# Fused forgetting attention and GELU MLP on one core: batch 2 in the order of the later batches

## The chip, the cores and the metric

The kernel runs on one core of a Trainium2 chip. The metric is device time in microseconds (us), the median of several runs. The engines are called as the profile calls them: PE (TensorE, matmuls), PEld (its weight loads), DVE (VectorE), ACT (ScalarE), POOL (GpSimd) and SP (SyncE). SP computes nothing here: its queue issues the DMAs of the outputs, of v, and all DMA transposes. POOL's queue issues the loads of q, k and the weights.

## The reference, cut to what matters

Two operations stand behind each other. The first is causal attention with a decay from a forget gate, the second a two-layer MLP with an exact GELU on its output.

```python
batch, n_heads, seq, head_dim = (8, 8, 576, 64)

def attention(q, k, v, f):
    B, H, S, D = q.shape
    scores = np.matmul(q, k.transpose(0, 1, 3, 2)) / np.sqrt(D)
    cum = np.cumsum(np.log(np.clip(f, 0.0001, 1.0)), axis=-1)
    decay = cum[:, :, :, None] - cum[:, :, None, :]
    causal = np.triu(np.ones((S, S), dtype=bool), k=1)
    scores = np.where(causal, -1000000000.0, scores + decay)
    scores = scores - np.max(scores, axis=-1, keepdims=True)
    attn = np.exp(scores)
    attn = attn / (np.sum(attn, axis=-1, keepdims=True) + 1e-09)
    return np.matmul(attn, v)

def mlp(x, w_in, w_out):             # x: 4608 tokens x 512, d_ff = 2048
    h = x @ w_in
    g = 0.5 * h * (1.0 + erf(h / np.sqrt(2.0)))
    return g @ w_out

a = attention(q, k, v, f)
out = mlp(a.transpose(0, 2, 1, 3).reshape(B * S, H * D), w_in, w_out)
```

## The kernel before, in words

The work goes batch by batch (b = 0 to 7), with the order of all instructions written out by hand. Of the 576 rows of a batch, 512 (TC) go through the MLP as one chunk; the other 64 (TL), its *tail*, are gathered over all eight batches in the tile `tails`, and go through the MLP together at the end.

A batch consists of these steps. `load_qk_tokens` (POOL's queue) and `load_v` (SP's queue, five DMAs) bring q, k and v. `transpose_dma` has SP transpose q and k of four heads into the tiles `tq` and `tk`, and `untangle` has DVE copy them into `qT[i]` and `kT[i]`, one pair of heads `i` at a time (L269). `weigh_v` multiplies v with the decay on POOL (L288). `scores(b, i, t)` computes four tiles of scores for a pair of heads (L319), takes their exponential on ACT (L329) and masks the diagonals on POOL (L331). `attend` multiplies with v (L350), `normalize` divides on DVE, and `x_dma` has SP transpose the result into `xT` (L397). The name "av" below stands for `attend` and `normalize` of a pair of heads, with its `x_dma`. `gemm1` is the first layer (L447) with the GELU on ACT (L467), 16 blocks of four matmuls.

The second layer of a batch is computed during the attention of the next one, as filling between the score tiles. It is a generator, and `take(fill, n)` runs `n` of its steps. In `gemm2_rows` (L551) a step is either one matmul over 128 rows ("n") or two matmuls of 64 rows that write two PSUM banks ("r"), which DVE then adds up (L565 copies one, L575 adds the other, L579 stores). A plan lists for each of four row blocks (`ts`) the PSUM pool that holds its banks and its 16 steps.

Batches 3 to 7 have one order: all 16 score tiles with filling between them (`FILL`), then `av(0)`, `av_both(1)`, `av_both(2)`, `av(3)`, four steps of filling, the tail (`tail` with 40 matmuls of L416, `tail_end` with a divide on DVE and a transpose on SP, L429), the rest of the filling, and `gemm1_open`, which opens seven PSUM banks as the transposed x of the four pairs arrive.

Batches 0 and 1 have orders of their own that the change leaves alone. Batch 2, too, has its own order. Its filling is longer by 48 steps (`gemm2_third`: 16 steps of `gemm2_second`, L615, and 32 of `PLAN_0` finish batch 0; then come 64 steps of batch 1 by `PLAN_1`). The av of pair `i - 1` stands behind the second score tile of pair `i`. It attends to five blocks of rows instead of four; the fifth holds the tail, which `x_tail` copies out of `xT` on POOL (L435). gemm1 opens with five blocks.

PSUM comes from three pools of two buffers each: `s_psum` (two banks a buffer, tag "s", scores), `o_psum` ("o") and `m_psum` ("m"). The pool `x_pool` has four buffers for each tag; the four x of a batch and the x of `tail_end` share the tag "x".

Of the kernel before, what the change touches and what calls it, by code (L numbers as in the profile page):

```python
# [54 lines left out]
def kernel(  # L55
# [18 lines left out]
    XC = NBLK * P  # L74
    TL = S - TC
    assert B * TL == TC
# [281 lines left out]
    def normalize(b, i, h):  # L358
        if (b, i) not in x_of:
            x_of[b, i] = x_pool.tile([P, NBLK, 2, D], BF16, tag="x", name="x")  # L360
        nm = blocks(b)
        divide(x_of[b, i][:, 0:nm, h, :], o_of[b, i, h], nm)

    def blocks(b):
        return NBLK if b in (0, 2) else NBLK - 1
# [11 lines left out]
    def xT(b):  # L377
        if b not in xT_of:
            xT_of[b] = xT_pool.tile([P, n_dm, XC], BF16, tag="xT", name="xT")
        return xT_of[b]  # L380

    def to_xT(b, i, copy, pool=m_psum, tag="m", ps=None):
        if ps is None:
            shape = [P, 2, 1024] if pool is s_psum else [P, XC]
            ps = pool.tile(shape, BF16, tag=tag, name="ps_x")
            if pool is s_psum:
                ps = ps[:, 0, 0:XC]
        nm = blocks(b)
        for m in range(nm):
# [3 lines left out]
        copy(xT(b)[:, i, 0 : nm * P], ps[:, 0 : nm * P])  # L393

    def x_dma(b, i):
        nm = blocks(b)
        nc.sync.dma_start_transpose(  # L397
            xT(b)[:, i, 0 : nm * P].rearrange("d (m p) -> d m p", p=P),
            x_of[b, i][:, 0:nm].rearrange("p m h d -> p (m h d)"),
        )  # L400
# [24 lines left out]
    def tail_end(b, o):  # L425
        x = x_pool.tile([P, NBLK, 2, D], BF16, tag="x", name="x")
        x = x.rearrange("p k h d -> p (k h) d")[:, 0:HP]
# [5 lines left out]

    def x_tail(b):
        nc.gpsimd.tensor_copy(tails[:, :, b], by_half(xT(b)[:, :, XC - TL :]))  # L435

# [40 lines left out]
    def gemm2(c):  # L477
# [43 lines left out]
    PLAN_0 = [(2, "o", 16 * "r"), (3, "m", 14 * "r" + 2 * "n")]  # L521
    PLAN_1 = [
        (0, "m", 14 * "r" + 2 * "n"),
        (1, "m", 14 * "r" + 2 * "n"),
        (2, "m", 12 * "r" + 4 * "n"),
        (3, "s", 16 * "n"),
    ]
# [3 lines left out]
    def gemm2_rows(c, plan):  # L531
# [4 lines left out]
        for ts, held, steps in plan:  # L536
            if held == "s":
                both = s_psum.tile([P, 2, d_model], FP32, tag="s", name="ps2")
                banks = [both[:, 0], both[:, 1]]
            else:  # L540
                pool = {"o": o_psum, "m": m_psum}[held]
                banks = [
                    pool.tile([P, d_model], FP32, tag=held, name="ps2")
                    for _ in range(2)
                ]
            ot = o_pool.tile([P, d_model], FP32, tag="ot", name="ot")
            for kt, step in enumerate(steps):
                last = kt == steps.rfind("r")
                for r in range(2 if step == "r" else 1):
# [5 lines left out]
                        start=kt == (steps.index("r") if r else 0),  # L555
# [4 lines left out]
                if "r" in steps and (kt == n_ff - 1 if held == "s" else last):  # L560
# [5 lines left out]
                if kt == n_ff - 1:  # L566
                    if "r" in steps:
                        sum_out(c, ts, ot, banks[0])
                    else:
                        nc.vector.tensor_copy(ot, banks[0])  # L570
                        store(c, ts, ot)
# [55 lines left out]
    def gemm2_third():  # L627
        yield from gemm2_second(0)
        yield from gemm2_rows(0, PLAN_0)
        yield from gemm2_rows(1, PLAN_1)  # L630
# [7 lines left out]
    def behind(t, h):  # L638

        g = x_pool.tile([P, 1], FP32, tag="gate", name="gate")  # L640
        nc.gpsimd.tensor_copy(g[:PT], t[:, h, 0:1])
# [196 lines left out]
    def gemm1_begin(b, both):  # L838
# [3 lines left out]
        to_xT(b, HP - 1, nc.vector.tensor_copy, ps=both[:, 1, 0:XC])  # L842
# [15 lines left out]
    FILL_2 = [[8, 8, 8, 8], [8, 8, 4, 4], [4, 4, 4, 4], [4, 4, 4, 4]]  # L858

    def av_both(b, i):  # L860
# [3 lines left out]
        nm = blocks(b)  # L864
        both = st[:, :, 0 : nm * (D + 1)].rearrange("p h (m d) -> p h m d", m=nm)
        for h in range(2):
            o_of[b, i, h] = both[:, h]
            attend(b, i, h, range(nm))
        x_of[b, i] = x_pool.tile([P, NBLK, 2, D], BF16, tag="x", name="x")
        r = x_pool.tile([P, 2, nm], FP32, tag="r2", name="r2")  # L870
        nc.vector.reciprocal(r, both[:, :, :, D])
        nc.vector.tensor_tensor(
            x_of[b, i][:, 0:nm].rearrange("p m h d -> p h m d"),
            both[:, :, :, 0:D],
            r.unsqueeze(3).to_broadcast([P, 2, nm, D]),
# [24 lines left out]
    def attention(b):  # L900
# [5 lines left out]
        def av(i, n=0):  # L906
            for h in range(2):
                attend(b, i, h, range(blocks(b)))
                normalize(b, i, h)
                if h == 0:  # L910
                    take(fill, n)
            x_dma(b, i)

        for i in range(HP):
            for t in range(4):
                scores(b, i, t)
                take(fill, counts[i][t])
                if t == 1 and b == 2 and i > 0:
                    av(i - 1)
                    if i == 1:  # L920
                        load_v(3)
# [3 lines left out]
                if b > 2 and i == 0 and t == 1:  # L925
                    load_v(b + 1)
                if b > 2 and t == 0 and i < 2:
                    transpose_dma(b + 1, 4 * i, 4 * i + 4)
                if b == 2 and t == 1 and i == 1:
                    transpose_dma(3, 0, 4)  # L930
        if b == 2:
            take(fill, 4)
            av(HP - 1)
        else:
            av(0)
            av_both(b, 1)
# [165 lines left out]
```

## Time and profile before

| | |
|---|---|
| median of 3 runs | 329.86 us (329.84 to 330.63) |
| the profiled execution's own time | 330.98 us |
| its span, first to last instruction | 329.3 us |
| PE busy | 317.3 us (96%) |
| DVE, ACT, POOL busy | 179.6, 203.1, 131.2 us |
| mean granted clock of PE | 0.999 |
| batch 2, first score matmul to that of batch 3 | 67.86 to 113.31 us |

All durations come from one profiled execution. A timeline line gives the start in us, the length in us, the engine, the line of the program, the operation, output and inputs, the shape, and how many instructions were merged; in brackets stands the idle time before it and what ended it. The length of a matmul includes its way through the array, so matmuls that follow each other overlap in the timeline, and the pace of a stream is read from the starts. Some per cent of the matmul records are missing, so a count can be one or two short. A window line gives the window, its length, and for each engine the busy time with the number of instructions, then the clock, the share of the DMA engines and their rate.

### The profile page before, as it was taken

The page shows a single profiled execution, that of the slowest core. Times are in us where ns is not written, and L with a number is a line of the kernel's source. Part 1 is how long each engine was busy: PE and PEld are TensorE (multiplying, and loading weights), DVE is VectorE, ACT ScalarE, POOL GpSimd, SP SyncE. Part 2 cuts the span into 40 slices and gives each one's busy share as a digit, 9 for nine tenths or more (in the row PEclk, how much of TensorE's full clock was granted, in tenths as well). Part 3 has the DMA queues.
Part 4 walks back from the last instruction along what each step waited for, and adds up shares of the span by engine and source line. Part 5 has one row for each costly group of instructions (what it writes and reads, how often), then busy time and mean ns, then how long its engine had stood idle before and what let it go on. Part 6 is the DMA issues. An engine that isn't in the chain of part 4 may idle for free.

```text
span 329.3 us, 8075 instructions
## 1 busy us (share of the span) xinstructions
PE 317.3 (96%) x3291; PEld 168.9 (51%) x3323; DVE 179.6 (55%) x424; ACT 203.1 (62%) x296; POOL 131.2 (40%) x254
## 2 busy tenths in 40 slices
PE   7999799999999999999999999999999999999995
PEld 3664445445554456445644565455545564444443
DVE  5852566584458935792599449953795270010011
ACT  4896785984635797189808990899178936405600
POOL 8996883019426153804471356225512510000000
PEclk9999999999999999999999999999999999999999
DMA  7999999988998999499959794969610131021012
GB/s 114 190 192 211 207 189 124 185 176 144 196 220 180 146 201 199 74 158 170 218 76 175 141 222 95 176 120 202 129 41 3 66 82 56 0 88 42 0 47 83
DMA packets 94117, 43.93 MB, mean 133 GB/s; under 512 B 73344, under 2 KB 88960, under 8 KB 94080
## 3 DMA queue, kind: packets, MB, share of 16 engines
q1 hardware_dynamic: 76928, 26.90, 41.1%
q0 software_dynamic: 16752, 15.99, 30.8%
q8 instruction: 26, 0.43, 0.6%
q10 hardware_dynamic: 400, 0.52, 0.4%
q14 instruction: 11, 0.09, 0.1%
HBM read 36.85 MB, written 9.44 MB: 141 GB/s over the span
## 4 chain that ended last, share of the span: by engine, by line
PE 84%; DMA 9%; POOL 3%; issue 1%; ACT 1%; DVE 0%; another core or an unknown queue 0%; POOLq 0%; DVEq 0%
PE ps L447 35%; PE ps L551 26%; PE ps L491 8%; PE s L319 6%; PE o L350 5%; DMA q<-in_k_dram 3%; DMA k<-in_k_dram 3%; DMA v_sb<-in_v_dram 2%; DMA xT<-x 1%; PE o L416 1%; PE ps L615 1%; ACT e L329 1%; POOL q L120 1%; POOL k L120 1%; POOL v_sb L169 1%
## 5 line engine op out<-in xcount | busy, mean ns | idle before, releaser
L467 ACT ACTIVATE g<-ps 128x512 bf16<-128x512 f32 x138 | 75.8, 616 | 85.5 <-PE ps L447 84.4
L447 PE MATMUL ps<-xT,w_in_sb 128*128 128x512 bf16 x498 | 112.8, 379 | 1.9 <-remote 0.3
L551 PE MATMUL ps<-w_out_sb,g 64*128 64x512 bf16 (+1 forms) x737 | 104.4, 376 | 0.8 <-issue 0.5
L329 ACT ACTIVATE e<-s 128x896 bf16<-128x896 f32 x112 | 87.8, 836 | 15.3 <-PE s L319 13.8
L447 PEld LDWEIGHTS <-w_in_sb 128*128 128x128 bf16 x576 | 55.0, 98 | 67.1 <-issue 3.2
L331 POOL TENSOR_SCALAR_AFFINE_SELECT e<-e 128x256 bf16<-128x256 bf16 (+1 forms) x135 | 49.2, 386 | 86.5 <-ACT e L329 86.4
L551 PEld LDWEIGHTS <-g 64*128 64x128 bf16 (+1 forms) x751 | 42.1, 94 | 31.3 <-issue 1.3
L288 POOL TENSOR_TENSOR vw<-v_sb,wT 128x640 bf16<-128x640 f32 (+1 forms) x30 | 38.1, 1272 | 34.7 <-DMA v_sb<-in_v_dram 18.6
L269 DVE COPY qT<-tq 64x288 bf16<-64x288 bf16 x96 | 43.0, 448 | 2.9 <-DMA tq<-q 1.4
L565 DVE COPY ot<-ps 128x512 f32<-128x512 f32 x20 | 13.8, 692 | 54.3 <-PE ps L551 54.3
L319 PE MATMUL s<-qT,kT 64*128 64x256 bf16 (+1 forms) x336 | 37.8, 275 | 0.8 <-DVE kT L241 0.6
L269 DVE COPY kT<-tk 64x288 bf16<-64x288 bf16 x96 | 35.4, 369 | 3.8 <-DMA tk<-k 2.1
L500 DVE COPY ot<-ps 128x512 f32<-128x512 f32 (+2 forms) x9 | 5.7, 632 | 49.5 <-PE ps L491 49.5
L319 PEld LDWEIGHTS <-kT 64*128 64x128 bf16 x336 | 18.1, 94 | 19.8 <-issue 4.0
L491 PE MATMUL ps<-w_out_sb,g 128*128 128x512 bf16 (+2 forms) x142 | 27.9, 355 | 0.1
L370 DVE TENSOR_TENSOR x<-o,r 128x256 bf16<-128x256 f32 (+1 forms) x51 | 22.2, 435 | 4.9 <-DMA xT<-x 3.3
L350 PEld LDWEIGHTS <-e 128*128 128x128 bf16 x600 | 20.2, 98 | 4.6 <-issue 2.1
L350 PE MATMUL o<-vw,e 128*128 128x65 bf16 x600 | 21.4, 194 | 0.2 <-POOL e L331 0.2
L491 PEld LDWEIGHTS <-g 128*128 128x128 bf16 x144 | 13.5, 98 | 14.5
L575 DVE TENSOR_TENSOR ot<-ot,ps 128x512 f32<-128x512 f32 x27 | 18.6, 688 | 3.0 <-remote 0.7
L447 PE MATMUL ps<-tails,w_in_sb 128*128 128x512 bf16 x64 | 14.3, 378 | 0.0
L670 ACT ACTIVATE e<-s 128x1024 bf16<-128x1024 f32 (+1 forms) x13 | 12.1, 990 | 2.1 <-PE s L665 1.9
(92 smaller groups left out, 192.0 us busy)
## 6 DMA issues: line engine op xcount, KB each, us to landing
out_dram<-ot SPq DMA_DIRECT2D x32, 256.0 KB, 2.7
v_sb<-in_v_dram SPq DMA_DIRECT2D x24, 256.0 KB, 4.8
q<-in_q_dram POOLq DMA_DIRECT2D x6, 576.0 KB, 7.0
k<-in_k_dram POOLq DMA_DIRECT2D x6, 576.0 KB, 9.5
v_sb<-in_v_dram POOLq DMA_DIRECT2D x17, 128.0 KB, 6.3
w_in_sb<-in_moe_w_in_dram POOLq DMA_DIRECT2D x4, 512.0 KB, 8.3
w_out_sb<-in_moe_w_out_dram POOLq DMA_DIRECT2D x4, 512.0 KB, 8.5
v_sb<-in_v_dram SPq DMA_DIRECT2D x6, 128.0 KB, 4.6
```

The lines of the kernel that those rows point to most:

```text
L269: nc.vector.tensor_copy(rows[:, odd], src[odd * D : (odd + 1) * D, 2 * i + h].rearrange("d j p -> d p j"),)
L288: eng.tensor_tensor(vw(b)[:, hs, n0:n1, 0:D], v_sb[:, hs, n0:n1, :], w.unsqueeze(3).to_broadcast([P, 2, n1 - n0, D]), Alu.mult,)
L319: nc.tensor.matmul(to, *ab, start=half < 0, stop=half == 1 or not masked)
L329: nc.scalar.activation(et[:, :, z:c], st[:, :, z:c], Act.Exp, scale=scale)
L331: nc.gpsimd.affine_select(out=et[:, :, c0 + z : c0 + P], in_=et[:, :, c0 + z : c0 + P], compare_op=Alu.is_ge, fill=0.0, base=z, pattern=[[ ...
L350: nc.tensor.matmul(o[:, m, :], e_of[b, i, t][:, h, c : c + P], vw_of[b][:, 2 * i + h, n, :], start=(n == 0), stop=(n == m),)
L370: nc.vector.tensor_tensor(x, o[:, 0:n, 0:D], r[:, 0:n].unsqueeze(2).to_broadcast([P, n, D]), Alu.mult,)
L447: nc.tensor.matmul(ps, w_in_sb[:, kt, ffb * P : (ffb + 1) * P], xT(c)[:, kt, 0:TC] if c < B else tails[:, kt % 2, :, kt // 2, :], start=(k ...
L467: nc.scalar.activation(g_of[c][ffb], ps, Act.Gelu)
L491: nc.tensor.matmul(pss[ts][:, c0:c1], g_of[c][kt][:, ts * P : (ts + 1) * P], w_out_sb[:, kt, c0:c1], start=(kt == 0), stop=(kt == n_ff - 1),)
L551: nc.tensor.matmul(banks[r], g_of[c][kt][rows, ts * P : (ts + 1) * P], w_out_sb[rows, kt, :], start=kt == (steps.index("r") if r else 0), ...
L575: nc.vector.tensor_tensor(ot, ot, bank, Alu.add)
```

## The change

Batch 2 takes the order of batches 3 to 7: four blocks of rows in every batch, the avs behind all score tiles, the tail by `tail` and `tail_end`, gemm1 by `gemm1_open` and the loop behind it from block 7 on. `blocks` and `x_tail` go, and so does `PLAN_1`: the second layer of batch 1 takes the `PLAN` of the others, and the last two steps of `PLAN_0` become row halves. `FILL_2` gives the steps of filling behind each score tile, 101 in all; the last 11 of the 112 steps follow the avs (four) and the tail (seven). On SP, `load_v(3)` stays behind the second score tile of pair 1, now ahead of any x; the transposes of q, k of heads 0 to 3 of batch 3 go behind the second score tile of pair 2, ahead of all x; those of heads 4 to 7 go behind the tail's transpose. In all batches the x of `tail_end` gets a tag of its own ("xt"), and `xT` holds 512 columns instead of 640.

The diff, cut to its core:

```diff
@@ -358,11 +358,7 @@
     def normalize(b, i, h):
         if (b, i) not in x_of:
             x_of[b, i] = x_pool.tile([P, NBLK, 2, D], BF16, tag="x", name="x")
-        nm = blocks(b)
-        divide(x_of[b, i][:, 0:nm, h, :], o_of[b, i, h], nm)
-
-    def blocks(b):
-        return NBLK if b in (0, 2) else NBLK - 1
+        divide(x_of[b, i][:, 0:NQ, h, :], o_of[b, i, h], NQ)
 
     def divide(x, o, n):
         r = x_pool.tile([P, NBLK], FP32, tag="r", name="r")
...
@@ -376,27 +372,25 @@
 
     def xT(b):
         if b not in xT_of:
-            xT_of[b] = xT_pool.tile([P, n_dm, XC], BF16, tag="xT", name="xT")
+            xT_of[b] = xT_pool.tile([P, n_dm, TC], BF16, tag="xT", name="xT")
         return xT_of[b]
 
     def to_xT(b, i, copy, pool=m_psum, tag="m", ps=None):
         if ps is None:
-            shape = [P, 2, 1024] if pool is s_psum else [P, XC]
+            shape = [P, 2, 1024] if pool is s_psum else [P, TC]
             ps = pool.tile(shape, BF16, tag=tag, name="ps_x")
             if pool is s_psum:
-                ps = ps[:, 0, 0:XC]
-        nm = blocks(b)
-        for m in range(nm):
+                ps = ps[:, 0, 0:TC]
+        for m in range(NQ):
             nc.tensor.transpose(
                 ps[:, m * P : (m + 1) * P], x_of[b, i][:, m, :, :], ident_bf
             )
-        copy(xT(b)[:, i, 0 : nm * P], ps[:, 0 : nm * P])
+        copy(xT(b)[:, i, 0:TC], ps[:, 0:TC])
 
     def x_dma(b, i):
-        nm = blocks(b)
         nc.sync.dma_start_transpose(
-            xT(b)[:, i, 0 : nm * P].rearrange("d (m p) -> d m p", p=P),
-            x_of[b, i][:, 0:nm].rearrange("p m h d -> p (m h d)"),
+            xT(b)[:, i, 0:TC].rearrange("d (m p) -> d m p", p=P),
+            x_of[b, i][:, 0:NQ].rearrange("p m h d -> p (m h d)"),
         )
 
     def tail(b):
...
@@ -423,16 +417,12 @@
         return o
 
     def tail_end(b, o):
-        x = x_pool.tile([P, NBLK, 2, D], BF16, tag="x", name="x")
-        x = x.rearrange("p k h d -> p (k h) d")[:, 0:HP]
+        x = x_pool.tile([P, HP, D], BF16, tag="xt", name="xt")
         divide(x, o, HP)
         nc.sync.dma_start_transpose(
             tails[:, :, b].rearrange("d i a t -> d i (a t)"),
             x.rearrange("p k d -> p (k d)"),
         )
-
-    def x_tail(b):
-        nc.gpsimd.tensor_copy(tails[:, :, b], by_half(xT(b)[:, :, XC - TL :]))
 
     def by_half(t):
         return t.rearrange("d (a i) t -> d i a t", a=2)
...
@@ -518,13 +508,7 @@
         (3, "m", 5 * "r" + 11 * "n"),
     ]
 
-    PLAN_0 = [(2, "o", 16 * "r"), (3, "m", 14 * "r" + 2 * "n")]
-    PLAN_1 = [
-        (0, "m", 14 * "r" + 2 * "n"),
-        (1, "m", 14 * "r" + 2 * "n"),
-        (2, "m", 12 * "r" + 4 * "n"),
-        (3, "s", 16 * "n"),
-    ]
+    PLAN_0 = [(2, "o", 16 * "r"), (3, "m", 16 * "r")]
 
     put_off = []
 
...
@@ -534,15 +518,10 @@
 
 
         for ts, held, steps in plan:
-            if held == "s":
-                both = s_psum.tile([P, 2, d_model], FP32, tag="s", name="ps2")
-                banks = [both[:, 0], both[:, 1]]
-            else:
-                pool = {"o": o_psum, "m": m_psum}[held]
-                banks = [
-                    pool.tile([P, d_model], FP32, tag=held, name="ps2")
-                    for _ in range(2)
-                ]
+            pool = {"o": o_psum, "m": m_psum}[held]
+            banks = [
+                pool.tile([P, d_model], FP32, tag=held, name="ps2") for _ in range(2)
+            ]
             ot = o_pool.tile([P, d_model], FP32, tag="ot", name="ot")
             for kt, step in enumerate(steps):
                 last = kt == steps.rfind("r")
...
@@ -552,23 +531,19 @@
                         banks[r],
                         g_of[c][kt][rows, ts * P : (ts + 1) * P],
                         w_out_sb[rows, kt, :],
-                        start=kt == (steps.index("r") if r else 0),
+                        start=kt == 0,
                         stop=last if r else kt == n_ff - 1,
                     )
                 if plan is PLAN and last and kt == n_ff - 1:
                     banks.reverse()
-                if "r" in steps and (kt == n_ff - 1 if held == "s" else last):
+                if last:
                     copy = partial(nc.vector.tensor_copy, ot, banks[1])
                     if plan is PLAN and ts == 3:
                         put_off.append(copy)
                     else:
                         copy()
                 if kt == n_ff - 1:
-                    if "r" in steps:
-                        sum_out(c, ts, ot, banks[0])
-                    else:
-                        nc.vector.tensor_copy(ot, banks[0])
-                        store(c, ts, ot)
+                    sum_out(c, ts, ot, banks[0])
                 yield
 
     def sum_out(c, ts, ot, bank):
...
@@ -627,7 +602,7 @@
     def gemm2_third():
         yield from gemm2_second(0)
         yield from gemm2_rows(0, PLAN_0)
-        yield from gemm2_rows(1, PLAN_1)
+        yield from gemm2_rows(1, PLAN)
 
     def take(gen, n):
         for _ in range(n):
...
@@ -855,24 +830,23 @@
 
 
     FILL = [[8, 4, 3, 3], [3, 3, 3, 3], [3, 3, 3, 3], [3, 3, 3, 2]]
-    FILL_2 = [[8, 8, 8, 8], [8, 8, 4, 4], [4, 4, 4, 4], [4, 4, 4, 4]]
+    FILL_2 = [[8, 8, 8, 8], [8, 8, 8, 7], [5, 5, 5, 5], [5, 5, 6, 2]]
 
     def av_both(b, i):
 
 
         st = s_psum.tile([P, 2, 512], FP32, tag="s", name="o2")
-        nm = blocks(b)
-        both = st[:, :, 0 : nm * (D + 1)].rearrange("p h (m d) -> p h m d", m=nm)
+        both = st[:, :, 0 : NQ * (D + 1)].rearrange("p h (m d) -> p h m d", m=NQ)
         for h in range(2):
             o_of[b, i, h] = both[:, h]
-            attend(b, i, h, range(nm))
+            attend(b, i, h, range(NQ))
         x_of[b, i] = x_pool.tile([P, NBLK, 2, D], BF16, tag="x", name="x")
-        r = x_pool.tile([P, 2, nm], FP32, tag="r2", name="r2")
+        r = x_pool.tile([P, 2, NQ], FP32, tag="r2", name="r2")
         nc.vector.reciprocal(r, both[:, :, :, D])
         nc.vector.tensor_tensor(
-            x_of[b, i][:, 0:nm].rearrange("p m h d -> p h m d"),
+            x_of[b, i][:, 0:NQ].rearrange("p m h d -> p h m d"),
             both[:, :, :, 0:D],
-            r.unsqueeze(3).to_broadcast([P, 2, nm, D]),
+            r.unsqueeze(3).to_broadcast([P, 2, NQ, D]),
             Alu.mult,
         )
         x_dma(b, i)
...
@@ -903,65 +877,39 @@
         fill = gemm2_third() if b == 2 else gemm2_rows(b - 1, PLAN)
         counts = FILL_2 if b == 2 else FILL
 
-        def av(i, n=0):
+        def av(i):
             for h in range(2):
-                attend(b, i, h, range(blocks(b)))
+                attend(b, i, h, range(NQ))
                 normalize(b, i, h)
-                if h == 0:
-                    take(fill, n)
             x_dma(b, i)
 
         for i in range(HP):
             for t in range(4):
                 scores(b, i, t)
                 take(fill, counts[i][t])
-                if t == 1 and b == 2 and i > 0:
-                    av(i - 1)
-                    if i == 1:
-                        load_v(3)
                 if b == 2 and (i, t) == (0, 3):
                     weigh_v(b, 2)
                     weigh_v(b, 3)
-                if b > 2 and i == 0 and t == 1:
+                if (i, t) == ((1, 1) if b == 2 else (0, 1)):
                     load_v(b + 1)
-                if b > 2 and t == 0 and i < 2:
-                    transpose_dma(b + 1, 4 * i, 4 * i + 4)
-                if b == 2 and t == 1 and i == 1:
-                    transpose_dma(3, 0, 4)
+                if (i, t) == ((2, 1) if b == 2 else (0, 0)):
+                    transpose_dma(b + 1, 0, 4)
+                if b > 2 and (i, t) == (1, 0):
+                    transpose_dma(b + 1, 4, 8)
+        av(0)
+        av_both(b, 1)
+        av_both(b, 2)
+        av(3)
+        take(fill, 4)
+        tail_end(b, tail(b))
         if b == 2:
-            take(fill, 4)
-            av(HP - 1)
-        else:
-            av(0)
-            av_both(b, 1)
-            av_both(b, 2)
-            av(3)
-            take(fill, 4)
-            tail_end(b, tail(b))
-            put_off.pop()()
-        if b == 2:
-            take(fill, 4)
-            transpose_dma(3, 4, 8)
+            transpose_dma(b + 1, 4, 8)
+        put_off.pop()()
         take(fill, 999)
-
-        if b == 2:
-            pss = [gemm1(b, ffb, (0, 1)) for ffb in range(2)]
-            pss += [spare(), spare()]
-            for ffb in range(2):
-                gemm1(b, ffb, (2,), pss[ffb])
-            for ffb in (2, 3):
-                gemm1(b, ffb, (0, 1, 2), pss[ffb])
-            for ffb in range(4):
-                gemm1(b, ffb, (3,), pss[ffb])
-            more = s_psum.tile([P, 2, 512], FP32, tag="s", name="ps1")
-            gemm1(b, 4, ps=more[:, 0, :])
-        else:
-            gemm1_open(b)
+        gemm1_open(b)
         if b + 1 < B:
             untangle(b + 1, 0)
             weigh_v(b + 1, 0)
-        if b == 2:
-            x_tail(b)
 
     def second_attention():
 
...
@@ -1037,8 +985,8 @@
         for ffb in range(4 if b < 2 else 5, n_ff):
             if b == 0 and ffb in HELD:
                 continue
-            aside = ffb in ((7, 8) if b == 2 else (8, 9, 12, 13)) if b > 1 else b == 1 and ffb % 4 < 2
-            if b <= 2 or ffb > 6:
+            aside = ffb in (8, 9, 12, 13) if b > 1 else b == 1 and ffb % 4 < 2
+            if b < 2 or ffb > 6:
                 gemm1(b, ffb, ps=spare() if aside else None)
             if b == 1 and ffb % 2 == 0:
                 at = HELD[(ffb - 4) // 2]
```

More of the change, by code (lines that the diff above doesn't have):

```diff
@@ L73 @@
     n_sub = TC // P
-    XC = NBLK * P
     TL = S - TC
+    NQ = TC // P
     assert B * TL == TC
@@ L640, in behind @@
         g = x_pool.tile([P, 1], FP32, tag="gate", name="gate")
-        nc.gpsimd.tensor_copy(g[:PT], t[:, h, 0:1])
+        nc.gpsimd.tensor_copy(g[:PT], t[:PT, h, 0:1])
     e0_of = {}
@@ L841, in gemm1_begin @@
         pss = [gemm1(b, ffb, (0, 1)) for ffb in range(2)]
-        to_xT(b, HP - 1, nc.vector.tensor_copy, ps=both[:, 1, 0:XC])
+        to_xT(b, HP - 1, nc.vector.tensor_copy, ps=both[:, 1, 0:TC])
         more = s_psum.tile([P, 2, 512], FP32, tag="s", name="ps1")
@@ L971, in av @@
         def av(i, h):
-            attend(b, i, h, range(blocks(b)))
+            attend(b, i, h, range(NQ))
             normalize(b, i, h)
@@ L1022, in second_attention @@
         both = s_psum.tile([P, 2, 1024], BF16, tag="s", name="ps_x2")
-        to_xT(b, 2, nc.scalar.copy, ps=both[:, 0, 0:XC])
+        to_xT(b, 2, nc.scalar.copy, ps=both[:, 0, 0:TC])
         av(3, 1)
```

## The prediction

> **What bounds the kernel now.** I read the page first, for the engine that is busy and the engine on the chain that ended last.
>
> ```profile
> PE 317.3 (96%) x3291; PEld 168.9 (51%) x3323; DVE 179.6 (55%) x424; ACT 203.1 (62%) x296; POOL 131.2 (40%) x254
> PE 84%; DMA 9%; POOL 3%; issue 1%; ACT 1%; DVE 0%; another core or an unknown queue 0%; POOLq 0%; DVEq 0%
> ```
>
> TensorE (PE) is the bound: 96% busy, 84% of the chain. Time is won only by giving PE fewer or denser matmuls, or by taking away something that PE waits for. The profiled execution took 330.98 us: its span is 329.3, and 1.7 lie around it. The median of the runs is 329.86, which is 1.1 less. I work out differences within the profiled span and take them off the median.
>
> Next I cut the span at the first score matmul of each batch (67.86, 113.31, ... in the timeline of PE) and asked for the busy time in these windows.
>
> ```profile
> core 0: us, PE busy (x) PEld busy (x) DVE busy (x) ACT busy (x) POOL busy (x), PEclk, DMA share, GB/s
> 67.86:113.31 45.45, 44.87 (x427) 22.71 (x432) 30.08 (x66) 25.11 (x35) 22.24 (x41) 1.00 1.04 182
> 113.31:147.67 34.36, 33.91 (x347) 18.34 (x349) 23.25 (x56) 23.46 (x34) 14.69 (x30) 1.00 0.84 153
> 181.68:215.68 34.00, 33.84 (x349) 18.49 (x351) 23.66 (x56) 23.47 (x34) 14.75 (x30) 1.00 0.79 154
> 215.68:249.85 34.17, 33.86 (x349) 18.35 (x351) 22.68 (x58) 23.46 (x34) 13.09 (x28) 1.00 0.62 119
> ```
>
> The rows are batches 2, 3, 5 and 6. A later batch takes 34.0 us; batches 3 and 6 take 0.36 and 0.17 more. The clock is 1.00 everywhere. Batch 2 has the same work and 48 more gemm2 steps (16 of gemm2_second, 32 of PLAN_0). The timeline of PE then shows what the two orders look like, first around one av of batch 2, then all avs of batch 5.
>
> ```profile
> 89.00 0.59 PE L551 MATMUL ps<-w_out_sb,g 64*128 64x512 bf16 x4
> 89.75 0.38 PE L551 MATMUL ps<-w_out_sb,g 128*128 128x512 bf16 x1 [0.16 <-issue]
> 89.97 1.11 PE L350 MATMUL o<-vw,e 128*128 128x65 bf16 x30
> 91.22 1.03 PE L551 MATMUL ps<-w_out_sb,g 64*128 64x512 bf16 x8
> ...
> 195.99 2.69 PE L350 MATMUL o<-vw,e 128*128 128x65 bf16 x80
> 198.73 0.81 PE L551 MATMUL ps<-w_out_sb,g 128*128 128x512 bf16 x3
> 199.47 0.84 PE L416 MATMUL o<-vw,e 128*64 128x65 bf16 x40
> 200.25 1.47 PE L551 MATMUL ps<-w_out_sb,g 128*128 128x512 bf16 x6
> 201.77 2.54 PE L447 MATMUL ps<-xT,w_in_sb 128*128 128x512 bf16 x11
> ```
>
> **The change, part by part.**
>
> PE, by whole batches. A step of two half-row matmuls ("r") takes 0.216: eight matmuls, four steps, run from 80.62 to the next scores at 81.48, 0.86. So the new batch 2 should take 34.00 + 48 x 0.216 = 44.37, against 45.45: **-1.08**.
>
> The same by parts. Four avs of five blocks took from 89.97 to the scores at 91.02, 1.05 each, 4.20; now 80 matmuls from 195.99 to 198.73 (2.74) and 40 of the tail from 199.47 to 200.25 (0.78), together 3.52: -0.68. The fifth block covered 128 rows of which 64 were wanted; the tail writes two heads at once at 19 ns a matmul. Before each of three avs the step from half-row to whole matmuls shows 0.16 of "issue"; one such step stays, so two go: -0.3. The opening of gemm1 and the rest of gemm1 took 99.32 to 113.31, 13.99, against 13.91 in batch 5: -0.08. The sum, -1.06, agrees.
>
> Fifteen steps turn from one whole matmul ("n") into two halves. Whole matmuls with a new weight load each run at 13.91 / 64 = 217 ns, a pair of halves at 216: nothing. A rule of the Trainium skill would say otherwise: the page "TensorE: Matmul & The Clock Gate", Part 3, The mechanism, says that a weight load overlaps matmuls in flight only where their row groups differ. By it each of the fifteen would save a load (94 to 98 ns in the groups), 1.5 us more; the 217 ns of this trace speak against it.
>
> VectorE (DVE). Four divides of 0.69 (0.19 + 0.49) a pair and a late copy take other shapes; DVE is busy 30 of 45 us and PE waits for it only through PSUM banks. The tightest is at av(0): five steps and a score tile lie between the end of ts 2 and av(0), 1.22 us, where later batches have 1.41 (two tiles). In batch 5 the second bank was free at 196.15 and wanted at about 196.33. So 0 to 0.1 is lost here; I take 0.
>
> ScalarE: a score tile now comes every 1.25 us (five steps and the scores) instead of 0.82, while one exponential takes 0.84: no cost. The sequence of gelus becomes that of batch 5.
>
> GpSimd (POOL): x_tail (0.43, after 4.87 waiting for xT) goes. What is queued behind it, three weigh_v and the q, k loads of batch 4 (issued at 104.98), moves up to about 101: in batch 3 the q load is issued 4.4 after the tail's end, which will be at 96.8. These loads then run while q, k of heads 4 to 7 of batch 3 are transposed (issued about 102 instead of 100.87). A transpose beside such loads landed 6.5 after its issue (x at 81.93), where 2.4 is the median, so they may land at 110 instead of 105.9. DVE's 16 copies (0.33 each) then end at 115.4. They are wanted by the scores of head pair 2 at 119, and DVE's next copy out of PSUM at 116.6. That cover hides it; without it the excess over 1.2 us would be paid.
>
> The tails' own tile: the tail's divide waited 1.45, 0.50 and 1.31 for the first x transpose (batches 3, 5, 6) because its buffer was that x's. PE did not wait: the wide PSUM tile was wanted only as gemm1 opened, and that waits for the same transpose. Gain 0 to 0.05; I take 0.
>
> SyncE (SP), the uncertain part. Before, in batch 2, and in batch 5:
>
> ```profile
> 83.32 7.13 SPq L134 DMA_DIRECT2D v_sb<-in_v_dram  x5
> 90.55 2.24 SPq L255 DMA_TRANSPOSE tq<-q  x1
> 92.89 1.32 SPq L255 DMA_TRANSPOSE tk<-k  x1
> ...
> 193.56 1.65 SPq L255 DMA_TRANSPOSE tk<-k  x1
> 195.30 1.25 SPq L579 DMA_DIRECT2D out_dram<-ot  x2
> 197.76 6.02 SPq L397 DMA_TRANSPOSE xT<-x  x4
> ```
>
> The new order is v, a store, q, k, two stores, then four x. The v loads wait for weigh_v of batch 2, which ends on POOL at 81.4, so they issue 1.9 earlier and take 4.8 to 7.1 us: until 86.2 to 88.5. A store (0.6), q and k (3.6) and two stores (1.1) end at 91.5 to 93.8. PE reaches av(0) at 67.86 + 16 tiles x 0.1725 + 101 x 0.216 + 0.1 = 92.5, and the first x is divided 1.75 later, at 94.3: SP is free. From av(0) to gemm1 batch 5 needs 5.78, so x(0) must be there by 98.2, 3.9 after its issue; the later batches took 2.3 to 4.1. **PE waits 0 to 0.65** (the upper end: transfers counted as one row behind v's last landing of before, 93.9; with q, k, three stores and x at 2.3, 0.8, 3 x 0.6 and 0.56 less the old x's 0.6, it lands at 98.8). I take 0.1, since batch 5 has this very order and waited nothing.
>
> Batches 3 and 6. There PE waited for x(0), once under an unnamed releaser:
>
> ```profile
> 133.41 0.23 another core or an unknown queue
> ```
>
> x(0) issued at 129.55 and landed only at 133.61; the DMA records have 16 KB of instructions fetched at 131.3, between its two ends (batch 6: at 232.7). The new batch 2 issues 30 more PE instructions (15 matmuls, 15 weight loads), so these fetches come up to 1 us earlier against x. Their 0.53 may vanish, or another batch may be hit as hard: -0.53 to +0.5. Earlier is better for both rows seen; I take -0.2.
>
> Sum: -1.08 + 0.1 - 0.2 = -1.18, so **328.7 us**.
>
> **The rivals.**
>
> B, x(0) lands late. For it: DMA share is 1.34 of nominal from 88 to 94, all that stands ahead of x. Wait 0.65, nothing from batches 3 and 6: -0.43, 329.4. Against it: batch 5. Chance 0.14.
>
> C, slower: the q, k transposes that now stand in front of x(0) on SP's queue run into the tail of the q, k loads and hold x. Before, x(0) went ahead of them. For it: one transpose of q, at 49 us beside weight loads, took 11.2 us to land instead of 4.3. At that price q issued at 87 to 89 lands at 98 to 100, k, two stores and x 2.6 later, at 101 to 103; PE waits 2.6 to 4.5 for a gain of 1.1, so +1.5 to +3.4: 331.4 to 333.3. It decides from a landing of x(0) after 99.3 (no gain) or 100.3 (0.3% slower). Against it: the k load had landed at 87.87, before either transpose is likely to start. Beside this: the Trainium skill, page "DMA: Bandwidth & Descriptors", Queues, rings and completion order, has each DMA engine consume a ring's descriptors in order, which speaks against putting q, k ahead of x; the x that took 6.5 us here agrees. Chance 0.13.
>
> D, the fetches come clear of x in batches 3 and 6 and x(0) of batch 2 is in time: -1.08 - 0.53 = -1.61, 328.3. Chance 0.11.
>
> E, weight loads are exposed in whole matmuls: fifteen more loads saved, 15 x 98 ns: -1.08 - 1.5, 327.3. Against it stand 217 ns in 64 matmuls. Chance 0.02.
>
> **How the numbers follow.** The forecast has 0.60. 0.3% (0.99 us) is about what a measurement of this kernel can tell from no change, and the forecast lies only 0.2 beyond it: of its 0.60 I put 0.43 beyond and 0.17 within. Faster: 0.43 + 0.11 + 0.02 = 0.56. Within: 0.17 + 0.14 = 0.31. Slower: 0.13. The range goes from D's 328.3 with DVE's and the fetches' spare 0.3, 328.0, to B with a wait that eats the whole gain, 330.0; C and E are left out.
>
> **What would show it.** Right: batch 2's window near 44.4; 80 L350 matmuls in one run near 92.5, then the tail's 40 and gemm1 5.8 later; L435 gone from POOL; the tail's divide without its wait. Wrong: idle PE ahead of L447 at 98 to 103 put down to xT (B up to 0.65, C above 1.1); pairs and whole steps at different pace (E); batch 3 longer than 34.4 with PE waiting for DVE copies of kT.

## The result and the profile after

The changed kernel takes **339.99 us** (median of six runs), the kernel before 330.04 in the same comparison: a ratio of 1.0305, with a 95% interval of 1.0272 to 1.0337. It is slower by 10 us, where 328.7 was forecast. Its profiled execution took 340.28 us, with a span of 338.6.

The page of the changed kernel first: busy time, chain, and the group of gemm1 (L437 is now the line of gemm1's matmul, L391 that of `x_dma`, L410 that of the tail, L530 that of `gemm2_rows`, L554 that of the store; L255, L269 and L350 are as before).

```profile
PE 320.0 (95%) x3308; PEld 169.6 (50%) x3338; DVE 181.6 (54%) x423; ACT 203.1 (60%) x296; POOL 131.3 (39%) x253
PE 85%; DMA 5%; DVE 4%; issue 2%; ACT 2%; SPq 1%; POOL 0%; DVEq 0%
L437 PE MATMUL ps<-xT,w_in_sb 128*128 128x512 bf16 x498 | 115.9, 386 | 10.8 <-DMA xT<-x 9.4
```

PE is busy 2.7 us longer and waits 9.4 us for transposed x ahead of gemm1, where almost nothing was before. The windows by batch (the rows are batches 2, 3 and 4, then two parts of batch 3) say where.

```profile
core 0: us, PE busy (x) PEld busy (x) DVE busy (x) ACT busy (x) POOL busy (x), PEclk, DMA share, GB/s
66.19:111.32 45.13, 44.26 (x444) 22.18 (x447) 25.89 (x52) 24.58 (x35) 21.73 (x40) 1.00 0.96 171
111.32:156.77 45.45, 37.17 (x348) 19.16 (x351) 29.39 (x70) 24.00 (x34) 15.14 (x30) 0.92 0.88 163
156.77:190.77 34.00, 33.84 (x348) 18.53 (x351) 22.25 (x50) 23.47 (x34) 14.76 (x30) 1.00 0.57 102
129.95:144.44 14.49, 6.32 (x32) 2.67 (x29) 13.67 (x31) 0.00 (x0) 7.43 (x10) 0.97 1.00 168
144.44:156.77 12.33, 12.27 (x43) 4.87 (x44) 2.23 (x7) 8.42 (x15) 0.00 (x0) 0.76 0.85 167
```

Batch 2, the one that was changed, went from 45.45 to 45.13. **Batch 3, whose PE work was not touched, went from 34.36 to 45.45.** The start of batch 2 came 1.67 earlier. That need not be the change's doing: with the code of the kernel before ahead of it, it came at 65.69 in another profile (late `x_tail`, below), against 67.86 in the profile shown ahead. Nor can the step from 45.45 to 45.13 be read closely: the old order of batch 2 took 46.70 and 46.78 in two other profiles (below), where PE waited 0.7 and 0.8 for DVE at its start. The differences of the spans add up: -1.67 ahead of batch 2, -0.32, +11.1 in batch 3, -0.17 in batch 6, and +0.4 behind the start of batch 7 make 9.3.

The timeline of PE shows the waits, first at the end of batch 2, then at the end of batch 3.

```profile
90.82 2.79 PE L350 MATMUL o<-vw,e 128*128 128x65 bf16 x80
94.40 0.84 PE L410 MATMUL o<-vw,e 128*64 128x65 bf16 x40
97.41 0.81 PE L437 MATMUL ps<-xT,w_in_sb 128*128 128x512 bf16 x3 [0.77 <-DMA xT<-x]
...
134.76 3.18 PE L437 MATMUL ps<-xT,w_in_sb 128*128 128x512 bf16 x14 [3.35 <-DMA xT<-x]
138.54 1.67 PE L437 MATMUL ps<-xT,w_in_sb 128*128 128x512 bf16 x7 [0.59 <-DMA xT<-x]
144.44 12.39 PE L437 MATMUL ps<-xT,w_in_sb 128*128 128x512 bf16 x42 [4.23 <-DMA xT<-x]
```

In batch 3 PE waits 3.35, 0.59 and 4.23: 8.2 us. After the last wait the granted clock is 0.76, and gemm1 takes 22.01 (134.76 to 156.77) instead of 13.91; less the two inner waits, 3.3 are left. Narrower windows show where:

```profile
core 0: us, PE busy (x), PEclk, DMA share, GB/s
134.00:143.00 9.00, 4.85 (x21) 1.00 1.03 149
144.44:150.44 6.00, 6.00 (x15) 0.50 0.75 156
150.44:156.77 6.33, 6.28 (x30) 1.00 0.94 177
```

Six microseconds at half the clock are 3.0 lost; the other 0.3 are lost at the two inner stops (the 14 and 7 matmuls ahead of them take 3.19 and 1.67, where 217 ns each would make 3.04 and 1.52). 8.2 less the 0.34 of before, and 3.3, are the 11.1. The 0.4 behind the start of batch 7 are a wait, too: there x(0), issued at 274.86, landed 4.3 later, with 16 KB of instructions fetched at 276.80 in its flight, and PE waited 0.51.

The stalls can be followed back through three queues. In the timeline of POOL the q load of batch 4 follows the third weigh_v:

```profile
99.45 0.32 POOL L295 CAST vw<-wT 128x10 bf16<-128x10 f32 x1
99.68 0.82 POOL L120 DMA_DIRECT2D q<-in_q_dram  x1
```

In the timeline of DVE the copies of head pair 2 of batch 3 wait for their transposes:

```profile
105.19 1.36 DVE L269 COPY kT<-tk 64x288 bf16<-64x288 bf16 x4
111.67 1.34 DVE L269 COPY qT<-tq 64x288 bf16<-64x288 bf16 x4 [5.13 <-DMA tq<-q]
113.03 1.36 DVE L269 COPY kT<-tk 64x288 bf16<-64x288 bf16 x4
114.42 1.68 DVE L269 COPY qT<-tq 64x288 bf16<-64x288 bf16 x4
116.13 1.62 DVE L269 COPY kT<-tk 64x288 bf16<-64x288 bf16 x4
```

And the timeline of SP, from those transposes to x of batch 3:

```profile
100.18 1.36 SPq L255 DMA_TRANSPOSE tq<-q  x1
101.59 4.32 SPq L255 DMA_TRANSPOSE tk<-k  x1
106.01 1.37 SPq L554 DMA_DIRECT2D out_dram<-ot  x1
116.13 1.29 SPq L255 DMA_TRANSPOSE tq<-q  x1
117.78 1.33 SPq L255 DMA_TRANSPOSE tk<-k  x1
119.21 5.90 SPq L134 DMA_DIRECT2D v_sb<-in_v_dram  x5
125.21 0.56 SPq L554 DMA_DIRECT2D out_dram<-ot  x1
125.81 1.62 SPq L255 DMA_TRANSPOSE tq<-q  x1
127.47 1.52 SPq L255 DMA_TRANSPOSE tk<-k  x1
129.12 1.83 SPq L554 DMA_DIRECT2D out_dram<-ot  x2
131.55 5.22 SPq L391 DMA_TRANSPOSE xT<-x  x4
```

The transposes issued at 100.18 and 101.59 landed at 111.65 and 112.54, 11.5 and 10.9 later. The last `qT` copies that read `tq` (114.42) end at 116.1, and in that moment SP issues the next transpose, that of batch 4, into the same buffer: `tq` and `tk` have one buffer each. SP had stood since 107.4, with v of batch 4, a store, two more transposes, two stores and x of batch 3 queued behind. x(0) goes out at 131.55, 5.9 after the first av of batch 3 began (125.69); before it was 1.9. And that late, x meets the next loads: POOL issues q, k of batch 5 at 134.45 and 135.25, and x(3), issued at 135.48, lands at 144.40, 8.9 us later, instead of 2.3 (134.38 to 136.69 before).

That is **theory T**: the loads of batch 4, let off early by the disappearance of `x_tail` from POOL, slow the transposes; the single buffer passes this on to SP's queue, SP to x, and x runs into the loads of batch 5. The rival, **theory R**, is that the transposes' new place behind the tails is late by itself. For batch 2's own loss a second theory, **T2**, is that the DMA queue in front of x is full with v, q and k; its rival, **R2**, is that x is late by its own transposes or by a fetch of instructions beside them.

### The profile page after: what moved, and what is told of

It is laid out like the page before. It is cut to its first block, busy times and chain, and to the rows that moved or that the text cites. A ratio compares the mean times of both kernels' runs of the same rounds, so it can differ in the third digit from the quotient of the medians.

```text
span 338.6 us, 8097 instructions
## 1 busy us (share of the span) xinstructions
PE 320.0 (95%) x3308; PEld 169.6 (50%) x3338; DVE 181.6 (54%) x423; ACT 203.1 (60%) x296; POOL 131.3 (39%) x253
## 4 chain that ended last, share of the span: by engine, by line
PE 85%; DMA 5%; DVE 4%; issue 2%; ACT 2%; SPq 1%; POOL 0%; DVEq 0%
PE ps L437 36%; PE ps L530 24%; PE ps L481 8%; PE s L319 6%; DMA xT<-x 5%; PE o L350 4%; PE ps_w L210 1%; SPq L391 1%; PE s L640 1%; PE ps L590 1%; DVE x L366 1%; PE ps_f L226 1%; PE o L410 1%; ACT e L329 1%; DVE kT L241 1%
## 5 line engine op out<-in xcount | busy, mean ns | idle before, releaser
L437 PE MATMUL ps<-xT,w_in_sb 128*128 128x512 bf16 x498 | 115.9, 386 | 10.8 <-DMA xT<-x 9.4
L530 PE MATMUL ps<-w_out_sb,g 64*128 64x512 bf16 (+1 forms) x754 | 104.5, 376 | 0.3
L437 PEld LDWEIGHTS <-w_in_sb 128*128 128x128 bf16 x576 | 55.9, 99 | 78.3 <-issue 14.6
L530 PEld LDWEIGHTS <-g 64*128 64x128 bf16 (+1 forms) x766 | 42.3, 94 | 30.9
L269 DVE COPY qT<-tq 64x288 bf16<-64x288 bf16 x96 | 44.5, 463 | 7.7 <-DMA tq<-q 6.2
L269 DVE COPY kT<-tk 64x288 bf16<-64x288 bf16 x96 | 35.5, 370 | 3.6 <-DMA tk<-k 1.9
L550 DVE TENSOR_TENSOR ot<-ot,ps 128x512 f32<-128x512 f32 x28 | 19.3, 688 | 4.1 <-remote 2.1
L350 PEld LDWEIGHTS <-e 128*128 128x128 bf16 x560 | 18.6, 98 | 3.9 <-issue 2.1
L350 PE MATMUL o<-vw,e 128*128 128x65 bf16 x560 | 19.8, 194 | 0.2 <-POOL e L331 0.2
L366 DVE TENSOR_TENSOR x<-o,r 128x256 bf16<-128x256 f32 x41 | 17.4, 425 | 1.4
L437 PE MATMUL ps<-tails,w_in_sb 128*128 128x512 bf16 x64 | 14.3, 378 | 0.0
```

The source lines that it names most:

```text
L269: nc.vector.tensor_copy(rows[:, odd], src[odd * D : (odd + 1) * D, 2 * i + h].rearrange("d j p -> d p j"),)
L350: nc.tensor.matmul(o[:, m, :], e_of[b, i, t][:, h, c : c + P], vw_of[b][:, 2 * i + h, n, :], start=(n == 0), stop=(n == m),)
L366: nc.vector.tensor_tensor(x, o[:, 0:n, 0:D], r[:, 0:n].unsqueeze(2).to_broadcast([P, n, D]), Alu.mult,)
L437: nc.tensor.matmul(ps, w_in_sb[:, kt, ffb * P : (ffb + 1) * P], xT(c)[:, kt, 0:TC] if c < B else tails[:, kt % 2, :, kt // 2, :], start=(k ...
L530: nc.tensor.matmul(banks[r], g_of[c][kt][rows, ts * P : (ts + 1) * P], w_out_sb[rows, kt, :], start=kt == 0, stop=last if r else kt == n_f ...
L550: nc.vector.tensor_tensor(ot, ot, bank, Alu.add)
```

## The experiments

**Hold the loads back** (changed kernel).

```diff
                 if ffb == (9 if b == 1 else 14):
+                    if b == 2:
+                        g = x_pool.tile([P, 1], FP32, tag="gate", name="gate")
+                        nc.gpsimd.tensor_copy(g, tq_of[3][1][:, H - 1, 0, 0:1])
                     load_qk_tokens(b + 2)
```

> The changed kernel, with POOL made to wait, ahead of the q, k loads of batch 4, for the landing of k's transpose of heads 4 to 7 (a copy of one column). Theory T (loads let off too early): in the changed kernel these loads were issued at 99.68, 0.5 us ahead of the transposes, which then took 11 us to land; late copies on DVE kept the single tq, tk buffer, SP's queue ran 4 us late through batch 3, its x came late and met the next q, k loads. By T batch 3 falls from 45.4 to 34.0 to 34.8 us and the time from 340.0 to 328.5 to 330. Theory R (the transposes' new place behind the tails is late by itself, whatever POOL does): batch 3 stays above 40 us, the time above 336.

Ratio 1.0049 (1.0020 to 1.0077) to the kernel before: of the 3% half a per cent is left. In its profile the loads are issued at 107.37, the transposes land 3.6 and 3.7 us after their issue, and batch 3 takes 36.16. R falls. The time of 331.99 lies above the 328.5 to 330 expected: T had asked for 34.0 to 34.8 in batch 3, and the loads, now held too long, landed at 116.8, SP's transpose of k waited for them at 116.95, and x(0) still came 2 us late, which PE waited out (1.62 and 0.37).

**The same cause without the change** (kernel before).

```diff
         if b == 2:
-            x_tail(b)
...
                     load_qk_tokens(b + 2)
+                if b == 2 and ffb == n_ff - 1:
+                    x_tail(b)
```

> The kernel before, with x_tail moved on POOL from the end of batch 2's attention to the end of its gemm1 loop, so that nothing holds back the q, k loads of batch 4; batch 2's order, its avs and its SP queue stay as before. T: the loads are issued near 100 instead of 104.98, the transposes of heads 4 to 7 (issued at 100.87) land near 111 instead of 105.9, batch 3's x comes late: 334 to 341 us. R: nothing of SP's order has changed, 330.0 (329.3 to 330.7).

Ratio 1.0101 (1.0035 to 1.0166). The timeline of SP in this kernel has the pattern of the changed one:

```profile
99.72 3.61 SPq L255 DMA_TRANSPOSE tq<-q  x1
103.38 4.48 SPq L255 DMA_TRANSPOSE tk<-k  x1
107.95 0.53 SPq L579 DMA_DIRECT2D out_dram<-ot  x1
116.07 1.30 SPq L255 DMA_TRANSPOSE tq<-q  x1
```

The loads went out at 98.50, the transposes landed at 111.81 and 112.69, SP stood until 116.07, and batch 3 took 36.62. So taking the wait off POOL makes the old order slower too, with batch 2's steps untouched. The size was missed by three of four runs (334 to 341 expected, 332.1 to 332.4 measured; the fourth, 336.89 at a granted clock of 0.994, was not profiled): in the profile x(0) came 2.60 late for PE, but the loads of batch 5 came behind the last x, so the second stall and the slower clock did not follow. The 0.43 us copy of `x_tail` had served as a gate.

**Cut the last link** (changed kernel): POOL waits in batch 3 for x(3), by the same three lines with `b == 3` and `xT(3)[:, HP - 1, 0:1]`.

> The changed kernel, with POOL made to wait in batch 3, ahead of the q, k loads of batch 5, for the landing of the last x transpose of batch 3. Only the last link of T's chain is cut: x(0) of batch 3 still comes 3 us late, but x(3) lands 2.4 us after its issue instead of 8.9. T: gemm1 of batch 3 falls from 22.0 to about 14.5, the time to 331.5 to 333.5. If the loss of batch 3 were SP's lateness alone, the time would stay at 339 to 341.

Its one execution took 335.8 us. x(3) landed 2.3 after its issue, as T says, and the second stall is gone. The time is 2 to 4 us above what was expected, since x(0) came even later (PE waited 3.95 for it) and gemm1 then took 15.55 at a clock of 0.89.

**Cut the middle link: tiles split by four heads** (changed kernel).

```diff
-                tq_pool.tile([P, H, JT // 2, PT], BF16, tag="t" + n, name=f"t{n}{b}")
+                [
+                    tq_pool.tile(
+                        [P, H // 2, JT // 2, PT],
+                        BF16,
+                        tag=f"t{n}{half}",
+                        name=f"t{n}{b}{half}",
+                    )
+                    for half in range(2)
+                ]
...
```

> The changed kernel, with the tiles of the transposed q and k split by halves of four heads, so that the transposes of heads 0 to 3 of batch 4 wait only for the copies of head pairs 0 and 1 of batch 3. The loads on POOL stay early, and the transposes of heads 4 to 7 of batch 3 still land near 111. The middle link of T is cut. T: those transposes are issued at the start of batch 3 (near 112 instead of 116.1), SP is in time, batch 3 takes 34.0 to 35.5 us, 328.7 to 330.5 in all. If late transposes of heads 4 to 7 cost directly (DVE or scores waiting), the time stays above 336.

Ratio 1.0033 (1.0003 to 1.0063). The loads stay early and the transposes of heads 4 to 7 still land at 112.70 and 113.50, but SP goes on:

```profile
101.15 1.71 SPq L263 DMA_TRANSPOSE tq<-q  x1
102.91 4.73 SPq L263 DMA_TRANSPOSE tk<-k  x1
107.74 0.73 SPq L562 DMA_DIRECT2D out_dram<-ot  x1
108.58 4.15 SPq L263 DMA_TRANSPOSE tq<-q  x1
...
129.16 6.21 SPq L399 DMA_TRANSPOSE xT<-x  x4
```

x(0) of batch 3 is issued 1.9 after the first av again, and batch 3 takes 34.74. Here late transposes are harmless by themselves; the buffer was the link. (The median, 330.81, lies 0.3 above what was expected.)

**One move on SP** (changed kernel): in batch 3, v of batch 4 ahead of the waiting transposes.

```diff
-                if (i, t) == ((2, 1) if b == 2 else (0, 0)):
+                if (i, t) == {2: (2, 1), 3: (0, 1)}.get(b, (0, 0)):
                     transpose_dma(b + 1, 0, 4)
```

> The changed kernel with one move: in batch 3, v of batch 4 is issued ahead of the transposes of heads 0 to 3 of batch 4 instead of behind them. Loads on POOL, late transposes of heads 4 to 7 and the single tq, tk buffer all stay. In the changed kernel SP stood from 107.4 to 116.1 before those transposes with v queued behind them. T (the loss is SP's queue standing behind one waiting instruction): the v loads fill that time, SP reaches x(0) of batch 3 in time, near 127.7, batch 3 takes 34.0 to 35.0, 329.0 to 330.5. If instead the transposes of batch 4 are what comes too late by themselves, or v now collides with the q, k loads: batch 3 stays above 38, the time above 333.

Ratio 1.0035 (1.0002 to 1.0069); batch 3 takes 34.54 in the profile. The v loads fill the time from 109.26 to 115.8, the transposes still come at 116.71, and x(0) is issued at 128.49, 1.9 after the first av. So the 10 us hung on SP's queue standing behind one waiting instruction. The median of 331.55 is still above the 329.0 to 330.5 expected.

**Transposes of heads 4 to 7 in front of x** (changed kernel): the second `transpose_dma` moved to (2, 1), behind the first.

> The changed kernel, with the transposes of heads 4 to 7 of batch 3 directly behind those of heads 0 to 3, in front of x, so that they meet no q, k loads. T: they land before 100, SP is in time in batch 3, which takes 34.0 to 34.8; x(0) of batch 2 goes 3 to 3.5 us later instead, start to gemm1 33.5 to 35: 331 to 333.5. If the loss of batch 3 hung on something else than these transposes' landing, batch 3 stays above 40.

Batch 3 takes 34.85, just above the 34.0 to 34.8 that T expected. The time, 335.6 for the one execution, was missed: it entered batch 2 only at 70.43, about 4 us later than the others, and batch 2 took 46.85 with waits of 1.64 and 0.69 for x. The stage says more here than the total.

**The tails' own tile alone** (kernel before).

```diff
-        x = x_pool.tile([P, NBLK, 2, D], BF16, tag="x", name="x")
-        x = x.rearrange("p k h d -> p (k h) d")[:, 0:HP]
+        x = x_pool.tile([P, HP, D], BF16, tag="xt", name="xt")
```

> The kernel before with one part of the change alone: the x of tail_end has its own tag and buffers. By the prediction's term and by T: nothing to PE, 330.1 (within 0.3%), only DVE's wait of up to 1.45 in the tail's divide goes. If sharing the buffer had a hidden use (holding back DVE's copies or a store), it is slower by more than 1 us. Its trace is also a second look at the old order of batch 2: start of batch 2 at 66 to 68, batch 2 45.4 to 46.7.

Ratio 1.0011 (0.9978 to 1.0044): nothing, as priced. Its trace has the old order of batch 2 take 46.78 from 66.42 to 113.20 (45.4 to 46.7 expected); PE waited 0.45 and 0.35 for DVE at its start.

**Where batch 2's gain went: no v** (split kernel).

```diff
-                    load_v(b + 1)
+                    if b > 2:
+                        load_v(b + 1)
```

> The split-tile kernel, with the five loads of v of batch 3 left out (v of batch 2 is used in their place, so batch 3 computes with the wrong v). It asks where the 1.08 us of batch 2 went: from batch 2's start to gemm1 the shared rows gave 30.46, the changed kernel took 31.2 and the split one 32.5, PE waiting for x(0). Theory T2 (the DMA queue in front of x is full with v, q, k and stores of this stretch): without v the wait goes, 30.4 to 30.7, batch 2 44.3 to 44.7, the time 328 to 329.5. Theory R2 (x is late by its own transposes or a fetch of instructions): still above 31.2, batch 2 above 45.

This kernel leaves out the loads of v for batch 3, which then works with v of batch 2. By the figures set beforehand it fell on R2's side: 31.56 from the start of batch 2 to gemm1 and 45.47 for the batch, against limits of 31.2 and 45. In part that is DVE, for which PE waited 0.27 and 0.35 early in batch 2. The end of the batch, a figure chosen afterwards, is cleaner. The timeline of PE without v, then with it (split kernel):

```profile
91.95 2.69 PE L358 MATMUL o<-vw,e 128*128 128x65 bf16 x80
97.73 1.46 PE L445 MATMUL ps<-xT,w_in_sb 128*128 128x512 bf16 x6
```

```profile
91.73 2.69 PE L358 MATMUL o<-vw,e 128*128 128x65 bf16 x80
99.01 1.24 PE L445 MATMUL ps<-xT,w_in_sb 128*128 128x512 bf16 x5 [1.56 <-DMA xT<-x]
```

From av(0) to gemm1 it takes 5.78, which is batch 5's figure of before, without v, and 7.28 with it. T2 holds for this stretch: without v in front of x, PE's wait of 1.56 is gone. A fetch of instructions lies in the flight of this x(0) in both (94.41 without v, 95.20 with it), so the fetch alone doesn't make the difference. In the total it brought nothing (330.95 us for the one execution).

**Two attempts to keep the gain** (split kernel). The first puts the transposes of heads 0 to 3 behind the tails, too, and holds the loads back to their landing; the second loads v of heads 4 to 7 behind the tails, with the loads issued ahead of the work on it.

```diff
         if b == 2:
+            transpose_dma(b + 1, 0, 4)
             transpose_dma(b + 1, 4, 8)
```

> The split-tile kernel, with the q, k transposes of heads 0 to 3 of batch 3, too, behind the tail's transpose instead of in front of x; POOL's q, k loads of batch 4 wait for the landing of the first of them; in batch 3 v of batch 4 goes ahead of the transposes of heads 0 to 3. T and T2: x(0) of batch 2 comes about 3 us earlier and PE's wait there goes (start to gemm1 30.4 to 30.8); batch 3 takes 34.0 to 35.0; 328.0 to 329.5. If the transposes, now three to four us later, hold up the copies for batch 3's first scores: PE waits at batch 3's start, and the time is 330 to 334.

```diff
-                    load_v(b + 1)
+                    load_v(b + 1, 0, H // 2 if b == 2 else H)
...
             transpose_dma(b + 1, 4, 8)
+            load_v(3, H // 2, H)
```

> The split-tile kernel, with v of batch 3 loaded in two halves: heads 0 to 3 where all of v was, heads 4 to 7 behind the transposes that follow the tail; POOL issues the q, k loads of batch 4 ahead of its work on the second half. T2: half of v is out of x's way, 2.7 us of DMA time, so PE's wait for x(0) in batch 2 (1.56 in the split kernel, 0 without any v) falls to 0 to 0.3; batch 3 keeps 34.4 to 34.9; 329.0 to 330.0, just faster than the kernel before (330.1). If the DMA queue through batch 3 is full as well, the second half of v and what stands behind it make x(0) of batch 3 late instead: batch 3 above 35.5, 330.5 to 333.

Both remove PE's wait for x in batch 2 (5.78 from av(0) to gemm1 in both; batch 2 takes 45.30 and 44.58). Both lose it in batch 3, which takes 37.95 and 35.77. In the first, the loads went out at 109.2 and landed at 120.1, the transposes behind them at 121.62, and PE waited 2.01 for x(0) and 1.4 for DVE; its profiled execution took 333.2 us, its four runs 331.7 to 340.7. In the second, PE waited for DVE, 0.76 at gemm1 of batch 3 and 0.42 before; ratio 1.0041 (1.0015 to 1.0067). Neither reached the time expected (328.0 to 329.5, 329.0 to 330.0). No version beat the kernel before.

## Why the prediction was wrong, point by point

- **PE's work: right, within 0.2.** 44.37 was worked out for batch 2. It took 45.13 with 0.77 of waiting for x, so 44.36. The kernel with half of v has no such wait and took 44.58. Whole and half-row steps run at the same pace; rival E is out.
- **The wait for x(0) in batch 2: the range was nearly right, the value not.** 0 to 0.65 was given and 0.1 taken, because batch 5 had this order and waited nothing; it was 0.77 in the changed kernel and 1.35 to 1.56 in four of its variants. SP had x(0) issued at 92.84, within 0.3 of the end of its divide, and it landed 4.44 later, behind what stood in the DMA queue, as rival B had it, with a fetch of instructions at 93.71 in its flight. Between the two profiles that alone would have left a gain of 0.3.
- **POOL's step failed, and with it the forecast.** It put the move of the loads at nothing. It had the loads move up to 101 (99.68), meet the transposes (they did), land these at 110 (111.65 and 112.54) and end the copies at 115.4 (117.7). The landing was priced with an x that took 6.5; the q that took 11.2, which rival C used, was the nearer row. (That q was issued at 53.69; the one at 49.40 landed in 4.1.) Then it asked only whether DVE and the scores were in time, and they were. It did not ask who waits for the *end of the copies*. SP does, for the single `tq` and `tk`; the row stood in the waits of SP before (transposes waiting for DVE's `qT` copies in four batches, 14.6 us). The cover of 1.2 was used up, as the copies ended 2.3 later than forecast, but the prediction named the wrong payer. It was not DVE or PE but SP's queue, which issued its next transpose 4.8 after the start of batch 3 (116.13) instead of 0.6 (113.93 before), and behind it x and the next loads: 11.1 us in batch 3. Of the sign set for this, a longer batch 3 came, but with PE waiting for `xT`, not for copies of `kT`.
- **Rival C named the right queue and the wrong place.** It had q, k hold x in batch 2, at 1.5 to 3.4 us. The holding came one batch later, through a buffer. In batch 2 q and k ahead of x landed 3.8 and 3.5 after their issue. The x that took 6.5 says nothing of the order within a queue: the k load beside it, until 87.87, was POOL's, on another queue.
- **The tails' tile: right** (1.0011). **Batches 3 and 6:** batch 6 took 34.00, its 0.17 gone as hoped, but batch 7 lost 0.4 with a fetch in the flight of its x(0), where none was before: the other outcome that the range allowed; in batch 3 the question was drowned. Without batch 3 the term of -0.2 came out as +0.2.
- **DVE at av(0):** 0 to 0.1 was given; the 80 matmuls took 2.84 (90.82 to 93.66) instead of 2.74.

What stays open: with the queue mended (split tiles, or v first) the kernel is level with the one before in the profile (spans of 329.3 and 328.5 against 329.3), yet 0.3% slower by the ratio of the runs. The start of gemm1 in batch 3 hardly moves: 133.75 before, 133.75 with split tiles, 133.18 with half of v, 132.88 with v first. In all of these x(0) of batch 3 lands 4.1 to 4.6 after its issue, and in all of them a fetch of instructions lies in its flight (131.29, 130.30, 129.99, 129.65). In batches 4 to 7 of the kernel before, x(0) took 2.3 and 2.3 without a fetch in its flight, 3.2 and 4.0 with one. That the traffic of this stretch, and no longer PE, sets that point is argued from these rows and not shown by an experiment; with half of v, PE's wait there was put down to DVE.

## What to carry to other kernels

When a wait disappears from a queue, list everything that was held behind it, and price those issues at their new time against every transfer in flight then: here the wait that was removed had kept two loads of 576 KB off two transposes. Follow a late transfer through the release of its buffer, not only to its first reader: the queue that refills the buffer stops, with all that stands behind it. PE time saved in one stage need not come back in the total, as in the kernels without v and with half of v, and a loss can show a batch later, in code that was not changed.

## What the runs showed of the hardware

- Transposes of q and k on SP's queue beside POOL's q, k loads took 11.5 and 10.9 us to land in the changed kernel (9.1 to 12.1 in the other kernels with early loads) instead of 3.5 and 3.7, and a transpose of x 8.9 instead of 2.3. In the DMA records of the changed kernel the loads moved 147 GB/s from 102 to 109 us, and SP's queue 34; with no data of the loads moving, SP's queue moved 222 GB/s from 101 to 106 in the kernel before.
- PE idle for 4.23 us cost 3.0 us more afterwards, at a clock of 0.50 until 150.44; 3.95 idle cost 1.6 (15.55 against 13.91 for gemm1, clock 0.50 for the first 3.36); 2.60 idle cost nothing (gemm1 13.92, in the kernel with the late `x_tail`). The Trainium skill, page "TensorE: Matmul & The Clock Gate", Part 1, has the clock fall to half after an idle window of about 3.4 us; these three rows agree.

The windows of the second row, in the kernel whose POOL waits for x(3):

```profile
core 0: us, PE busy (x), PEclk, DMA share, GB/s
136.59:139.95 3.36, 3.36 (x8) 0.50 0.37 83
139.95:152.14 12.19, 12.14 (x56) 1.00 1.00 168
```

In the changed kernel the first wait of batch 3, 3.35, left the clock at 1.00 up to 143 (windows above).
